# Summing q's shift row by one matmul of a high and a low part instead of a full-precision matmul, in a one-core transformer block

## The chip, the cores and the metric

The kernel is one launch on one core of a Trainium2 chip. The metric is device time in microseconds (us), the median of the runs shown. The core's engines are TensorE (PE in the rows; its weight loads are PEld), VectorE (DVE), ScalarE (ACT), GpSimd (POOL) and SyncE (SP), each with a queue that is worked off in order, and 16 DMA engines that serve transfers issued by SyncE, ScalarE and GpSimd. Instructions of different engines wait for one another through semaphores.

## The reference

A block of two parts on x with 2048 tokens (S) and 448 channels (D), all in float32. A condition vector c gives six rows of length 448 (shift, scale and gate for each part):

```python
mod = (silu(c) @ w_mod).reshape(1, 6, 1, -1)
sa, ca, ga, sb, cb, gb = (mod[:, i] for i in range(6))
h = layernorm(x) * (1 + ca) + sa
x = x + ga * A(h, wqkv, wo)       # linear attention, 16 heads of 28
h = layernorm(x) * (1 + cb) + sb
x = x + gb * B(h, w1, b1, w2, b2) # MLP over the tokens, 1792 wide
```

In A, q, k and v are h @ wqkv, phi(t) = where(t > 0, t + 1, exp(t)) + 1e-6, kv and z sum phi(k) v and phi(k) over the tokens, and the output is phi(q) kv / (phi(q) z), times wo.

## The kernel before

The 2048 tokens are 16 tiles of 128. float32 products are made of float32r matmuls: an operand is split into a high part (ScalarE's copy to float32r) and a low part (VectorE's difference), and three products high*high, high*low and low*high are added in PSUM. A matmul's moving operand has 448 columns.

**Projection with the norm folded in.** k and q are projected from the raw tile x (transposed by the host, `xt`), with weights scaled by 1 + ca (`Whi`, `Wlo`). Mean, and what the shift sa adds, enter by a last small matmul: `close(t, j)` (line 437) multiplies rows of tile t (mean and standard deviation, brought into place by a transpose on TensorE, `a_transpose`, line 401) with `Wrow[j]`, which holds the column sums of the scaled weights and the **shift row** sa @ W of projection j (j = 1 is k, j = 0 is q).

**How `Wrow[0]` is made.** `row_part(0, ch)` (line 275) adds, on VectorE, the four weight chunks times the shift column into `accb[0]`, [128, 448] float32. `row_sum(0)` (line 283) sums the weights' parts over the partitions by seven matmuls with the selector `sel_s`; `row_bias(0)` (line 289) adds the sum of `accb[0]` over its 128 partitions, by one matmul with float32 operands (`sel_b`, all 128 partitions). `row_out(0)` (line 292) copies the result's rows into `Wrow[0]` by ScalarE (high) and VectorE (low). `close(0, 0)`, q of tile 0, is the first that needs it.

**The order** is the program's own (a manual schedule): each engine gets its instructions in the order in which the code issues them. The loop over t from 4 to 15 (line 682) works on several tiles at once. In turn t, TensorE projects k of tile t+1, closes tile t, adds tile t-4 to the kv sums (`a_outer`, eleven matmuls, tiles `cacc`), transposes rows for tiles t+1 and t+2 (odd t) and, from t = 10 on, projects q of tile t-10 (`a_q`). VectorE and ScalarE take statistics of tile t+3, normalise tile t-2 (`a_norm`: tile `xn`; `a_high`, `a_low`: `xh`, `xl`), form phi(k) of tile t (`pk`), and split tile t+3 (`hh`, `hl`). `a_rows(t+2)` (line 393) writes on VectorE what the transpose reads (`rowst`). The third of the six rows, ga, is made beside it: `mod_part(2, k)`, k = 0 to 3, and `mod_add(2)` on VectorE, `mod_high(2)` on ScalarE and VectorE, then `mod_sum2(2)`, a matmul (tile `modp`), in turn 12.

GpSimd issues transfers that add to a tile in SBUF (`nc.gpsimd.dma_start(..., accum_op=ALU.add)`, lines 528 and 541): the low parts of phi(k), and the running sums of phi(k) for odd and even tiles. SyncE issues all loads. Temporaries come from a pool of 74 equal buffers (`slot`): a new tile takes a freed buffer, and its first writer waits for whoever used the buffer last.

After the loop come the attention output, tile by tile, interleaved with the first group of the MLP's first layer (lines 950 to 952), then the rest of that layer, and the second layer as seven products (lines 1183 and 1184).

Of the kernel before, what the change touches and what calls it, by code (L numbers as in the profile page):

```python
# [8 lines left out]
F32 = mybir.dt.float32  # L9
F32R = mybir.dt.float32r  # L10
AF = mybir.ActivationFunctionType
# [3 lines left out]
P = 128  # L15
S, D, F = 2048, 448, 1792
# [15 lines left out]
ROWS = 98  # L32
# [5 lines left out]
CUT2 = {2: 9, 3: 9, 4: 8, 5: 7}  # L38
LAG = 5
MOD_AT = {11: [(4, 0), (4, 1), (4, 2)], 13: [(4, 3), (4, None), (3, 0), (3, 1)]}  # L40
QS = {0: 3}
WARM = 6
POOL_LOW = (0, 1, 2)
# [8 lines left out]
def block_kernel(ctx: ExitStack, tc: tile.TileContext, x, xt, wqkv, wo, w1, b1, w2, c, wmod, wfirst, out):  # L52
    nc = tc.nc
# [5 lines left out]
    cst = ctx.enter_context(tc.tile_pool(name="cst", bufs=1))  # L59
# [16 lines left out]
    def moving(new, name, dt=F32R, parts=P):  # L76
        return new(name, dt=dt, parts=parts, w=512)[:, 16:16 + D]
# [22 lines left out]
        nc.gpsimd.affine_select(out=m3, in_=m3, compare_op=ALU.is_ge, fill=0.0, base=DH - 1,  # L100
                                pattern=[[0, 4], [DH, 4], [0, DH]], channel_multiplier=-1)

    cst.tile([P, 112], F32, name="space")
    mhalf = cst.tile([P, 2], F32, name="mhalf")
    nc.vector.memset(mhalf, -0.5)
    roots = cst.tile([P, 2], F32, name="roots")
# [2 lines left out]
    sel_b = cst.tile([P, ROWS], F32, name="sel_b")  # L109
# [3 lines left out]
    for i in (64, 66, 96):  # L113
        nc.gpsimd.memset(sel_f[:, i:i + 1], -1.0)
        nc.gpsimd.memset(sel_b[:, i + 1:i + 2], 1.0)
    sel_s = cst.tile([P, ROWS], F32R, name="sel_s")
    rowst = []
    for i in range(RING):
        rowst.append(cst.tile([P, P], F32R, name=f"rowst{i}"))
# [107 lines left out]
    def mod_part(j, k):  # L227
        if k == 0:
            macc[j] = (tslot if j == 5 else slot)(f"acc{j}", parts=G)
            nc.vector.tensor_scalar_mul(macc[j], wm[j, 0], sc[:G, 0:1])  # L230
        else:
            nc.vector.scalar_tensor_tensor(macc[j], wm[j, k], sc[:G, k:k + 1], macc[j], op0=ALU.mult, op1=ALU.add)


    def mod_add(j):
        acc = macc[j]
        nc.vector.tensor_add(acc[:G - 64], acc[:G - 64], acc[64:])

    def mod_high(j):
        acc, both = macc[j], moving(slot, f"mh{j}")  # L240
        macc[j] = (both,)
        nc.scalar.activation(both[:64], acc[:64], AF.Copy)
        return lambda: nc.vector.tensor_sub(both[64:], acc[:64], both[:64].bitcast(F32))
# [12 lines left out]
    Whi, Wlo, Wrow, rowb, accb = {}, {}, {}, {}, {}  # L256
# [18 lines left out]
    def row_part(j, ch):  # L275
        if ch == 0:
            accb[j] = slot(f"accb{j}")
            nc.vector.tensor_scalar_mul(accb[j], raw_w[j, 0], col[0][:, 0:1])
        else:
            nc.vector.scalar_tensor_tensor(accb[j], raw_w[j, ch], col[0][:, ch:ch + 1], accb[j],  # L280
                                           op0=ALU.mult, op1=ALU.add)

    def row_sum(j):
        rowb[j] = bank(f"rowb{j}")
        ws = [Whi[j, ch] for ch in range(4)] + [Wlo[j, ch] for ch in range(3)]
        for i, w in enumerate(ws):
            nc.tensor.matmul(rowb[j][:ROWS, :D], sel_s, w, start=(i == 0), stop=False)  # L287

    def row_bias(j):
        nc.tensor.matmul(rowb[j][:ROWS, :D], sel_b, accb.pop(j), start=False, stop=True)  # L290

    def row_out(j):
        ps, w = rowb.pop(j), Wrow[j]
        nc.scalar.activation(w[64:ROWS], ps[64:ROWS, :D], AF.Copy)
        nc.vector.tensor_sub(w[96:ROWS], ps[96:ROWS, :D], w[96:ROWS].bitcast(F32))
# [155 lines left out]
    def a_exp(t, ps):  # L451
        a_exp1(t, ps)
        a_relu(t, ps)
# [31 lines left out]
    def a_phi_q(keep=0):  # L485
        a_exp_q(keep)
        for t in sorted(eqs):
            pq[t] = phi_q(t)
# [191 lines left out]
    wo_sb = []  # L680
    late = [t for t in range(NT) if t not in Q_EARLY.values()]
    for t in range(4, NT):
        if 5 < t < NT - 1:
            project(t + 1, 1, "kp")
        kp = close(t, 1) if t > 4 else kps[4]
        if t == 9:
            row_sum(0)
            row_bias(0)
        if t > 4:
            a_outer(t - KV_LAG)  # L690
        if t % 2 and 4 < t < NT - 2:
            a_transpose(t + 1)
        if t in Q_EARLY:
            a_q(Q_EARLY[t])
        if t == 12:
            mp = mod_sum2(2)
        pair = t % 2 and 7 < t + 3 < NT
        if pair:
            first, second, end = a_stats_dve((t + 3, t + 4))
            first(0)  # L700
        if 5 <= t < 9:
            w_low(0, t - 5)
        if pair:
            second(0)
        if 5 <= t < 9:
            row_part(0, t - 5)
        a_phi_q(t in Q_EARLY)
        if t == 9:
            a_exp(t, kp)
        if t % 2 and 4 < t < NT - 2:  # L710
            a_copy(t + 1)
            a_copy(t + 2)
        if t != 9:
            a_exp(t, kp)
        if 7 < t + 3 < NT:
            a_split_high(t + 3)
        a_pk_parts(t - 1)
        highs = HIGH_AT.get(t, (t - 2,))
        for i in highs[:1]:
            a_norm(i)  # L720
            a_high(i)
        if t % 2 == 0 and 4 < t < NT - 3:
            low = a_rows(t + 2)
        if t == 11:
            low2 = mod_high(2)
        for j, i in MOD_AT.get(t, ()):
            mod_add(j) if i is None else mod_part(j, i)
        if t == 14:
            low4()
        a_pk(t, kp)  # L730
        if t % 2 == 0 and 4 < t < NT - 3:
            low()
        if 7 < t + 3 < NT:
            a_split_low(t + 3)
        for i in highs[1:]:
            a_norm(i)
            a_high(i)
        if pair:
            first(1)
        for i in highs:  # L740
            a_low(i)
        if pair:
            second(1)
            end()
        sum_end()
        if 4 <= t < 8:
            w_high(0, t - 4)
            if t == 7:
                w_row(0)
        if t == 9:  # L750
            row_out(0)
        if t == 12:
            mod_out(2, mp)
            make_mask()
        if t in FETCH:
            load_xt(FETCH[t])
            load_x(FETCH[t])
        if 7 <= t < 11:
            mod_part(2, t - 7)
        if t == 10:  # L760
            mod_add(2)
        if t == 11:
            low2()
        if t == 13:
            low4 = mod_high(4)
        if t in (7, 10):
            load_mod(4 if t == 7 else 3)
        if t == 10:
            load_qkv(2, tslot)
        if t == 8:  # L770
            for g in range(4):
                w = tslot(f"wo{g}", parts=G)
                nc.sync.dma_start(w, wo[g * G:(g + 1) * G, :])
                wo_sb.append(w)
            b12 = cst.tile([P, NF + NT], F32, name="b12")
            nc.sync.dma_start(b12, b1)
            b1c, b2c = b12[:, :NF], b12[:, NF:]
        if t >= 13:
            nc.vector.tensor_mul(wo_sb[t - 13], wo_sb[t - 13], mods[2][:G])
        load_to(PRE_LOAD.get(t, 0))  # L780
# [34 lines left out]
    for ch in range(4):  # L815
        for g in range(4):
            s = slice(g * G, (g + 1) * G)
            nc.tensor.matmul(kvb[:G, s], raw_w[2, ch][:, s], csum[ch][:, s], start=(ch == 0 and g == 0),  # L818
                             stop=(ch == 3), skip_group_check=True)
# [168 lines left out]
    for i in range(NT + LAG):  # L988
# [11 lines left out]
        t = i - LAG  # L1000
# [386 lines left out]
```

## Time and profile before

| what | before |
|---|---|
| median of 3 runs | 433.62 us (433.53 to 434.19) |
| the profiled execution | 434.09 us |
| its span, first to last instruction | 432.4 us |
| TensorE matmul busy | 427.9 us (99%) |
| VectorE busy | 365.1 us (84%) |
| ScalarE busy | 278.9 us (65%) |
| GpSimd busy | 120.1 us (28%) |
| moved by DMA | 66.14 MB, mean 153 GB/s |

The span is 1.69 us shorter than the profiled execution's time; what lies around the span is no instruction of the program. Times inside the profile count from the first instruction. In a row of the timeline stand the start, the duration, the engine, the source line, the operation, the tile written and those read, the shapes, the count, and in brackets how long the engine was idle before it and what ended that. Consecutive matmuls overlap in these rows (their ends are modelled), so their spacing is read from the starts.

### The profile page before, as it was taken

How to read it: one execution, taken by the hardware profiler on the slowest of the kernel's cores; microseconds unless marked ns; L12 is line 12 of the kernel's file. 1: busy time of each engine (PE TensorE's matmuls, PEld its weight loads, DVE VectorE, ACT ScalarE, POOL GpSimd, SP SyncE). 2: the span in 40 equal slices, each digit the busy share in tenths (PEclk: the TensorE clock that was granted, in tenths of full speed). 3: DMA queues.
4: the chain of work that ended last, by engine and by line, in shares of the span. 5: the costliest groups of instructions: out<-in, count | busy, mean ns of one | idle time of the engine just before them, and what ended most of it. 6: DMA issues, size and time to landing. Idle time of an engine off the chain costs nothing.

```text
span 432.4 us, 7216 instructions
## 1 busy us (share of the span) xinstructions
PE 427.9 (99%) x2331; PEld 398.0 (92%) x2331; DVE 365.1 (84%) x814; ACT 278.9 (65%) x595; POOL 120.1 (28%) x199
## 2 busy tenths in 40 slices
PE   8999999999999999999999999999999999999997
PEld 8888899999899999999999999999999999999996
DVE  4899987889899999998579695739799998898894
ACT  5799869658578899996755263537464664655550
POOL 4345444300026577775200000010113131132010
PEclk9999999999999999999999999999999999999999
DMA  8997997565300036354427461577379977986431
GB/s 282 385 337 162 239 264 162 89 206 193 86 1 0 26 74 148 74 125 97 145 85 244 142 212 50 166 203 210 79 193 214 207 159 159 214 170 144 85 46 41
DMA packets 63797, 66.14 MB, mean 153 GB/s; under 512 B 4816, under 2 KB 55312, under 8 KB 63760
## 3 DMA queue, kind: packets, MB, share of 16 engines
q1 hardware_dynamic: 54688, 50.90, 37.8%
q0 software_dynamic: 8784, 14.32, 20.8%
q10 hardware_dynamic: 288, 0.46, 0.4%
q8 instruction: 18, 0.29, 0.3%
q14 instruction: 19, 0.16, 0.1%
HBM read 46.30 MB, written 7.34 MB: 124 GB/s over the span
## 4 chain that ended last, share of the span: by engine, by line
PE 97%; DVE 1%; ACT 1%; issue 0%
PE y L1183 19%; PE up L951 10%; PE up L950 10%; PE up L952 10%; PE y L1184 9%; PE cacc L554 7%; PE qp L432 7%; PE op L893 7%; PE kp L432 6%; PE op L900 1%; PE warm L188 1%; PE tq L863 1%; PE qp L439 1%; PE kvb L818 1%; PE wp L968 1%; PE rowb L287 1%
## 5 line engine op out<-in xcount | busy, mean ns | idle before, releaser
L950 PE MATMUL up<-h2h,ph 128*128 128x448 f32 x224 | 81.2, 362 | 0.0
L951 PE MATMUL up<-h2l,ph 128*128 128x448 f32 x224 | 81.2, 362 | 0.0
L952 PE MATMUL up<-h2h,pl 128*128 128x448 f32 x224 | 80.8, 361 | 0.0
L1138 POOL DMA_DIRECT2D a<-a x16 | 14.2, 964 | 142.6 <-DMA pr<-in_B_w_dram 76.7
L950 PEld LDWEIGHTS up<-h2h,ph 128*128 128x128 f32 x224 | 42.0, 188 | 3.1
L952 PEld LDWEIGHTS up<-h2h,pl 128*128 128x128 f32 x224 | 41.9, 187 | 3.0
L951 PEld LDWEIGHTS up<-h2l,ph 128*128 128x128 f32 x224 | 42.0, 188 | 2.3
L84 DVE TENSOR_TENSOR pl<-pr,ph 128x512 fp32r<-128x512 f32 x46 | 30.7, 688 | 2.6 <-ACT ph L83 1.7
L1189 ACT ACTIVATE cc<-y 128x448 f32<-128x448 f32 x24 | 13.0, 546 | 26.7 <-PE y L1184 26.7
L1102 DVE TENSOR_TENSOR u<-u,mod 128x448 f32<-128x448 f32 x14 | 8.7, 623 | 23.0 <-ACT u L1101 22.8
L83 ACT ACTIVATE ph<-pr 128x512 fp32r<-128x512 f32 x46 | 27.6, 623 | 0.8 <-PE up L952 0.5
L1101 ACT ACTIVATE u<-up,b 128x448 f32<-128x448 f32 x14 | 8.8, 625 | 25.4 <-PE up L952 24.9
L432 PE MATMUL kp<-wh,hh 128*128 128x448 f32 x64 | 23.8, 377 | 0.0
L554 PE MATMUL cacc<-pkh,xh 128*128 128x448 f32 x64 | 23.6, 369 | 0.0
L432 PE MATMUL qp<-wh,hh 128*128 128x448 f32 x64 | 23.5, 368 | 0.0
L1203 POOL DMA_DIRECT2D out_dram<-yt x14 | 12.7, 909 | 37.3 <-DVE yt L1194 27.9
L843 POOL TENSOR_SCALAR den<-den 128x16 f32<-128x16 f32 x16 | 8.8, 548 | 44.2 <-DVE den L840 44.2
L554 PE MATMUL cacc<-pkl,xh 128*128 128x448 f32 x56 | 20.3, 362 | 0.0
L893 PE MATMUL op<-wph,pth 128*128 128x448 f32 x48 | 18.7, 390 | 0.0
L1144 DVE TENSOR_TENSOR a<-a,s 128x512 f32<-128x512 f32 (+1 forms) x32 | 18.5, 622 | 0.0
L83 ACT ACTIVATE s2h<-s 128x512 fp32r<-128x512 f32 (+1 forms) x16 | 8.3, 569 | 15.5 <-DVE s L1144 15.5
L1183 PE MATMUL y<-ub,a11h 128*128 128x448 f32 x56 | 18.2, 375 | 0.0
(235 smaller groups left out, 1383.7 us busy)
## 6 DMA issues: line engine op xcount, KB each, us to landing
pr<-in_B_w_dram SPq DMA_DIRECT2D x56, 256.0 KB, 3.1
a<-in_B_w_dram SPq DMA_DIRECT2D x32, 256.0 KB, 4.8
a<-in_B_w_dram SPq DMA_DIRECT2D x32, 192.0 KB, 4.7
xt<-in_xt_dram SPq DMA_DIRECT2D x16, 256.0 KB, 5.0
x<-in_A_x_dram SPq DMA_DIRECT2D x16, 224.0 KB, 5.0
wm<-in_B_wmod_dram SPq DMA_DIRECT2D x16, 196.0 KB, 5.2
out_dram<-x SPq DMA_DIRECT2D x14, 224.0 KB, 2.3
out_dram<-yt POOLq DMA_DIRECT2D x14, 224.0 KB, 6.1
```

The lines of the kernel that those rows point to most:

```text
L83: nc.scalar.activation(hi, full, AF.Copy)
L84: nc.vector.tensor_sub(lo, full, hi.bitcast(F32))
L432: nc.tensor.matmul(pps[t, j][:, :D], a[:, ch * P:(ch + 1) * P], w, start=first, stop=False)
L554: nc.tensor.matmul(cacc[ch][:, :D], a[:, s], b, start=(t == 0 and i == 0), stop=(t == NT - 1 and i == len(todo) - 1))
L893: nc.tensor.matmul(opb[t][:, :D], a, b, start=(ch == n == 0), stop=False)
L950: nc.tensor.matmul(ps[:, :D], hi[:, sl], mh, start=first, stop=False)
L951: nc.tensor.matmul(ps[:, :D], hi[:, sl], ml, start=False, stop=False)
L952: nc.tensor.matmul(ps[:, :D], lo[:, sl], mh, start=False, stop=last)
L1138: nc.gpsimd.dma_start(w, a, accum_op=ALU.add)
L1144: nc.vector.tensor_tensor(w, raw2[q, a][i], raw2[q, b][i], op=op)
L1183: nc.tensor.matmul(ps[:, :D], h[:, s], w, start=opens and r == 0, stop=False, skip_group_check=True)
L1184: nc.tensor.matmul(ps[:, :HD], l[:, s], wh, start=False, stop=closes and r == PAIRS - 1, skip_group_check=True)
```

## The change

`accb[0]` is no longer summed by the float32 matmul. In turn 8, after the last `row_part(0, 3)`, `row_fold(0)` adds, on VectorE, partitions 64 to 127 of `accb[0]` to its partitions 0 to 63 (64x448). In turn 9 `row_high(0)` copies the 64 partitions' high part by ScalarE into a new tile `rb0` (float32r, rows 0 to 63), copies the selector to float32r (`sel_r`, also ScalarE), and VectorE writes the low part into rows 64 to 127. `row_bias(0)` becomes one float32r matmul of `sel_r` with `rb0`. Its place and that of `row_sum(0)` move from turn 9 (after `close(9, 1)`) to the start of turn 10, ahead of the projection of tile 11; `row_out(0)` moves from the end of turn 9 to turn 10, after `close(10, 1)`. The steps `mod_part(2, 1..3)` and `mod_add(2)` move from turns 8, 9, 10 and 10 to turns 9, 10, 11 and 11. The spacer tile in the constants' pool shrinks by what `sel_r` takes. k's shift row (j = 1) stays as it was.

```diff
+PARTS = (7, 9, 10)
...
-    cst.tile([P, 112], F32, name="space")
+    cst.tile([P, 14], F32, name="space")
...
+    sel_r = cst.tile([P, ROWS], F32R, name="sel_r")
...
     def row_bias(j):
-        nc.tensor.matmul(rowb[j][:ROWS, :D], sel_b, accb.pop(j), start=False, stop=True)
+        nc.tensor.matmul(rowb[j][:ROWS, :D], sel_r if j == 0 else sel_b, accb.pop(j), start=False, stop=True)
+
+    def row_fold(j):
+        acc = accb[j]
+        nc.vector.tensor_add(acc[:64], acc[:64], acc[64:])
+
+    def row_high(j):
+        acc, both = accb[j], moving(slot, f"rb{j}")
+        nc.scalar.activation(both[:64], acc[:64], AF.Copy)
+        nc.scalar.activation(sel_r, sel_b, AF.Copy)
+        accb[j] = both
+        return lambda: nc.vector.tensor_sub(both[64:], acc[:64], both[:64].bitcast(F32))
...
     for t in range(4, NT):
+        if t == 10:
+            row_sum(0)
+            row_bias(0)
         if 5 < t < NT - 1:
             project(t + 1, 1, "kp")
         kp = close(t, 1) if t > 4 else kps[4]
-        if t == 9:
-            row_sum(0)
-            row_bias(0)
+        if t == 10:
+            row_out(0)
...
         if 5 <= t < 9:
             row_part(0, t - 5)
+            if t == 8:
+                row_fold(0)
         a_phi_q(t in Q_EARLY)
         if t == 9:
             a_exp(t, kp)
+            row_high(0)()
...
         if t == 11:
+            mod_part(2, 3)
+            mod_add(2)
             low2 = mod_high(2)
...
-        if t == 9:
-            row_out(0)
...
-        if 7 <= t < 11:
-            mod_part(2, t - 7)
-        if t == 10:
-            mod_add(2)
+        if t in PARTS:
+            mod_part(2, PARTS.index(t))
```

The order of the instructions on three stretches, before and now; numbers behind a name are buffers, and in brackets stand the semaphores that an instruction waits for (DVE is VectorE's own, DMASW are GpSimd's transfers). Line numbers of the changed kernel are 2 to 16 higher.

VectorE in turn 8, before: the last part of the shift row, then `xn` of tile 6, the two writes of `rowst` for tile 10's transpose, `mod_part(2, 1)` (`acc`), and the statistics of tile 12.

```order
L280 SCALAR_TENSOR_TENSOR accb_561<-wr_3_175,col_199,accb_561 128x448
L496 TENSOR_SCALAR xn_770<-x_167,mv_486 128x448
L395 CAST rowst_105<-mv_677 128x4x2 [waits Pool_49]
L458 SCALAR_TENSOR_TENSOR pk_776<-ek_758,rk_759 128x448 [waits Activation_49]
L398 TENSOR_TENSOR rowst_105<-mv_677,rowst_105 128x2x2 [waits DVE_49]
L415 TENSOR_TENSOR hl_763<-xt_536,hh_762 128x512 [waits DMAHW3_49,Activation_49]
L505 TENSOR_TENSOR xh_772<-xn_770,xh_772 128x64 [waits DMASW6_49,DMASW5_49,Activation_49]
L506 TENSOR_TENSOR xl_773<-xn_770,xh_772 128x384
L232 SCALAR_TENSOR_TENSOR acc_723<-wm_1_374,sc,acc_723 112x448 [waits DMAHW6_49]
L380 BN_STATS st_830<-x_597 128x6 [waits DMAHW6_49]
L383 BN_AGGR mv_828<-st_830 128x2 [waits DVE_49]
L496 TENSOR_SCALAR xn_847<-x_179,mv_486 128x448
```

The same stretch now:

```order
L282 SCALAR_TENSOR_TENSOR accb_562<-wr_3_176,col_200,accb_562 128x448
L296 TENSOR_TENSOR accb_562<-accb_562 64x448 [waits DVE_49]
L509 TENSOR_SCALAR xn_772<-x_168,mv_487 128x448 [waits DVE_49]
L408 CAST rowst_106<-mv_678 128x4x2 [waits Pool_49]
L471 SCALAR_TENSOR_TENSOR pk_778<-ek_760,rk_761 128x448 [waits Activation_49]
L411 TENSOR_TENSOR rowst_106<-mv_678,rowst_106 128x2x2 [waits DVE_49]
L428 TENSOR_TENSOR hl_765<-xt_537,hh_764 128x512 [waits DMAHW3_49,Activation_49]
L518 TENSOR_TENSOR xh_774<-xn_772,xh_774 128x64 [waits DMASW6_49,DMASW5_49,Activation_49]
L519 TENSOR_TENSOR xl_775<-xn_772,xh_774 128x384
L393 BN_STATS st_822<-x_598 128x6 [waits DMAHW6_49]
L396 BN_AGGR mv_820<-st_822 128x2 [waits DVE_49]
L303 TENSOR_TENSOR rb_829<-accb_562,rb_829 64x448 [waits Activation_49]
```

The fold (L296) stands ahead of `rowst`, with a wait for VectorE's own last result before and behind it; the low part of `rb0` (L303) stands behind tile 12's first statistics; `mod_part(2, 1)` is gone from here.

TensorE around the row matmuls, before: after tile 9's close, the seven sums, the float32 matmul, and the first kv matmul of tile 5 (ten more follow, and then the transpose `rw` and tile 11's projection).

```order
L287 MATMUL rowb_806<-wh_3_715,sel_s 98x448 [waits DVE_49]
L287 MATMUL rowb_806<-wl_0_558,sel_s 98x448
L287 MATMUL rowb_806<-wl_1_622,sel_s 98x448
L287 MATMUL rowb_806<-wl_2_681,sel_s 98x448
L290 MATMUL rowb_806<-accb_561,sel_b 98x448 [waits DVE_49]
L554 MATMUL cacc_437<-pkh_632,xh_701 128x448
```

Now they stand behind tile 5's kv matmuls and the transpose:

```order
L567 MATMUL cacc_441<-pkl_634,xh_702 128x448
L417 MATMUL rw_818<-ident,rowst_106 98x128 [waits DVE_49]
L289 MATMUL rowb_864<-wh_0_535,sel_s 98x448 [waits Activation_49]
L289 MATMUL rowb_864<-wh_1_594,sel_s 98x448
L289 MATMUL rowb_864<-wh_2_651,sel_s 98x448
L289 MATMUL rowb_864<-wh_3_716,sel_s 98x448
L289 MATMUL rowb_864<-wl_0_559,sel_s 98x448
L289 MATMUL rowb_864<-wl_1_623,sel_s 98x448
L289 MATMUL rowb_864<-wl_2_682,sel_s 98x448
L292 MATMUL rowb_864<-rb_829,sel_r 98x448 [waits DVE_49,Activation_49]
L445 MATMUL kp_873<-wh_0_223,hh_764 128x448
```

Eight matmuls moved back behind eleven others and the transpose, so those twelve come earlier; the transpose waits for `rowst`, the last row matmul for `rb0`.

VectorE in turn 11, before: phi(q) of tile 0, `xn` of tile 9, three parts of the fifth row (`mod_part(4, 0..2)`), phi(k) of tile 11, and the rest of the turn.

```order
L470 SCALAR_TENSOR_TENSOR pq_998<-eq_994,rq_995 128x448 [waits PE_49,Activation_49]
L496 TENSOR_SCALAR xn_1014<-x_370,mv_554 128x448
L230 TENSOR_SCALAR acc_1021<-wm_0_725,sc 112x448 [waits DMAHW1_49,PE_49]
L232 SCALAR_TENSOR_TENSOR acc_1021<-wm_1_727,sc,acc_1021 112x448 [waits DMAHW2_49,DVE_49]
L232 SCALAR_TENSOR_TENSOR acc_1021<-wm_2_729,sc,acc_1021 112x448 [waits DVE_49]
L458 SCALAR_TENSOR_TENSOR pk_1025<-ek_1002,rk_1003 128x448 [waits PE_49,Activation_49]
L415 TENSOR_TENSOR hl_1007<-xt_865,hh_1006 128x512 [waits DMAHW2_49,Activation_49]
L380 BN_STATS st_1028<-x_932 128x6 [waits DMAHW5_49]
L505 TENSOR_TENSOR xh_1016<-xn_1014,xh_1016 128x64 [waits DMASW6_49,DMASW5_49,Activation_49]
```

Now:

```order
L483 SCALAR_TENSOR_TENSOR pq_1002<-eq_998,rq_999 128x448 [waits PE_49,Activation_49]
L509 TENSOR_SCALAR xn_1018<-x_371,mv_555 128x448 [waits DMASW6_49,DMASW5_49]
L234 SCALAR_TENSOR_TENSOR acc_724<-wm_3_379,sc,acc_724 112x448
L239 TENSOR_TENSOR acc_724<-acc_724 48x448 [waits DVE_49]
L232 TENSOR_SCALAR acc_1027<-wm_0_726,sc 112x448 [waits DMASW1_49,DMAHW1_49,DVE_49,PE_49]
L234 SCALAR_TENSOR_TENSOR acc_1027<-wm_1_728,sc,acc_1027 112x448 [waits DMAHW2_49,DVE_49]
L234 SCALAR_TENSOR_TENSOR acc_1027<-wm_2_730,sc,acc_1027 112x448 [waits DVE_49]
L471 SCALAR_TENSOR_TENSOR pk_1031<-ek_1006,rk_1007 128x448 [waits Activation_49]
L428 TENSOR_TENSOR hl_1011<-xt_859,hh_1010 128x512 [waits DMAHW2_49,Activation_49]
```

Two steps of the third row came in ahead of the fifth's. And since the buffers of the pool fall to other tiles, the wait for GpSimd's transfers DMASW6 and DMASW5 (phi(k) of tile 9 added to the odd tiles' sum, and its low part) has gone from `xh` of tile 9, seven places further on, to `xn` of tile 9 itself.

## Prediction

> **What bounds the kernel now.** I read the page's busy times and its chain first: which engine is full, and whose work ended last.
>
> ```profile
> PE 427.9 (99%) x2331; PEld 398.0 (92%) x2331; DVE 365.1 (84%) x814; ACT 278.9 (65%) x595; POOL 120.1 (28%) x199
> ...
> PE 97%; DVE 1%; ACT 1%; issue 0%
> ```
>
> TensorE is busy for 99% of the span and makes up 97% of the chain. Then the waits of TensorE, the whole view:
>
> ```profile
> PE warm L188 <- DVE roots L108: 1.1, 1, 1.1
> PE rw L404 <- ACT rk L449: 0.2, 1, 0.2
> ```
>
> Two waits, 1.3 us in all. So a microsecond that TensorE saves or loses in the middle is saved or lost at the end, unless a wait moves in. Next, TensorE's own rows at the place (starts; a long row merges its count).
>
> ```profile
> 48.90 0.97 PE L287 MATMUL rowb<-wh,sel_s 128*98 128x448 f32 x4
> ...
> 50.32 0.91 PE L290 MATMUL rowb<-accb,sel_b 128*98 128x448 f32 x2
> ...
> 51.27 0.37 PE L554 MATMUL cacc<-pkl,xh 128*128 128x448 f32 x1
> ...
> 53.29 0.27 PE L404 MATMUL rw<-ident,rowst 128*98 128x128 f32 x1
> ...
> 53.60 0.36 PE L432 MATMUL kp<-wl,hh 128*128 128x448 f32 x1
> ```
>
> The seven float32r sums take 50.32 - 48.90 = 1.42 us, 0.20 each. The float32 matmul (two rows) and the first kv matmul end at 51.27, so 0.95 - 0.20 = 0.75 for the float32 one. Ten more kv matmuls bring us from 51.27 to 53.29: eleven are 2.22. Transpose and one matmul are 0.31, the transpose 0.11; the first matmul of tile 11's projection stands at 53.60 - 0.20 = 53.40.
>
> The engine that feeds TensorE here is VectorE; its timeline in turn 8:
>
> ```profile
> 49.01 0.69 DVE L280 SCALAR_TENSOR_TENSOR accb<-wr,col,accb 128x448 f32<-128x448 f32 x1
> 49.61 0.51 DVE L496 TENSOR_SCALAR xn<-x,mv 128x448 f32<-128x448 f32 x1
> ...
> 50.64 0.16 DVE L398 TENSOR_TENSOR rowst<-mv,rowst 128x4 fp32r<-128x4 f32 x1
> ...
> 51.45 0.55 DVE L506 TENSOR_TENSOR xl<-xn,xh 128x384 fp32r<-128x384 f32 x1
> 51.92 0.68 DVE L232 SCALAR_TENSOR_TENSOR acc<-wm,sc,acc 112x448 f32<-112x448 f32 x1
> 52.51 0.62 DVE L380 BATCH_NORM_STATS2 st<-x 128x6 f32<-128x448 f32 x1
> 53.17 0.18 DVE L383 BATCH_NORM_AGGREGATE mv<-st 128x2 f32<-128x6 f32 x1
> ```
>
> No row carries an idle time: VectorE works without a pause here, so whatever is put in delays all that stands behind it. `rowst`, which the transpose reads, is complete at 50.80, and the transpose runs at 53.29: a lead of 2.5 us, most of it because the row matmuls stand in between.
>
> **The change part by part.** *The saved matmul.* One float32r matmul replaces 0.75 by 0.20: TensorE gains 0.55 us. No other TensorE work is added. That alone would put tile 11's first matmul at 53.40 - 0.55 = 52.85.
>
> *The row matmuls go behind the transpose.* Tile 5's kv matmuls start at 48.90 and end their turn at 48.90 + 2.22 = 51.12, where the transpose is due.
>
> *The fold on VectorE.* Two later stretches of VectorE show its price and that of everything behind (turns 10 to 12):
>
> ```profile
> 61.00 0.68 DVE L232 SCALAR_TENSOR_TENSOR acc<-wm,sc,acc 112x448 f32<-112x448 f32 x1
> 61.72 0.62 DVE L237 TENSOR_TENSOR acc<-acc 48x448 f32<-48x448 f32 x1
> ...
> 63.54 0.51 DVE L496 TENSOR_SCALAR xn<-x,mv 128x448 f32<-128x448 f32 x1
> 64.44 0.45 DVE L230 TENSOR_SCALAR acc<-wm,sc 112x448 f32<-112x448 f32 x1 [0.40 <-PE cacc L554]
> 64.93 1.41 DVE L232 SCALAR_TENSOR_TENSOR acc<-wm,sc,acc 112x448 f32<-112x448 f32 x2
> 66.54 0.62 DVE L458 SCALAR_TENSOR_TENSOR pk<-ek,rk 128x448 f32<-128x448 f32 x1 [0.20 <-ACT rk L449]
> 67.08 0.69 DVE L415 TENSOR_TENSOR hl<-xt,hh 128x512 fp32r<-128x512 f32 x1
> 67.69 0.62 DVE L380 BATCH_NORM_STATS2 st<-x 128x6 f32<-128x448 f32 x1
> 69.04 0.23 DVE L505 TENSOR_TENSOR xh<-xn,xh 128x64 fp32r<-128x64 f32 x1 [0.73 <-ACT xh L500]
> ...
> 70.06 0.62 DVE L243 TENSOR_TENSOR mh<-acc,mh 64x448 fp32r<-64x448 f32 x1
> 70.71 0.63 DVE L470 SCALAR_TENSOR_TENSOR pq<-eq,rq 128x448 f32<-128x448 f32 x1
> ```
>
> `mod_add` (L237) is the same kind of fold: 0.62 us, started 0.04 after the end of what it reads. `row_fold` then runs from 49.01 + 0.69 + 0.04 = 49.74 to 50.36, and `xn`, which now waits for it, starts at 50.40 instead of 49.61: 0.79 later, and so does all behind it. The moved `mod_part(2, 1)` gives nothing back here, as it stood behind `rowst`. So `rowst` is complete at 50.80 + 0.79 = 51.59, after 51.12.
>
> What a late operand costs TensorE shows in turn 1 of the kv sums: the chain, then TensorE's rows.
>
> ```profile
> 30.19 0.48 DVE xl L506
> 30.67 0.04 issue
> ```
>
> ```profile
> 30.71 0.47 PE L554 MATMUL cacc<-pkh,xl 128*128 128x448 f32 x1
> 31.02 0.37 PE L554 MATMUL cacc<-pkh,xh 128*128 128x448 f32 x1
> ```
>
> The matmul starts 0.04 after VectorE's result, and the next follows after 0.31 instead of 0.20: I count 0.05 and then 0.10. The transpose starts at 51.64 and has lost 51.64 + 0.10 - 51.12 = 0.62 us. With 0.11 for itself and 1.42 for the sums, the last row matmul is due at 53.27.
>
> *The low part of `rb0`.* Its form is L243's (64x448, written to the upper partitions): 0.62, starting 0.03 after its forerunner. `xl` of tile 6 starts at 51.45 + 0.79 = 52.24; the statistics follow after 0.47 (their place, 51.92, is free of `mod_part`) at 52.71; the aggregate after 0.66 at 53.37, to 53.55; the low part runs from 53.58 to 54.20. ScalarE must have written the high part by then. Its rows:
>
> ```profile
> 50.17 0.56 ACT L500 ACTIVATE xh<-xn 128x448 fp32r<-128x448 f32 x1
> 50.63 0.62 ACT L446 ACTIVATE ek<-kp,mv 128x448 f32<-128x448 f32 x1
> 51.15 0.63 ACT L449 ACTIVATE rk<-kp,mv 128x448 f32<-128x448 f32 x1
> ```
>
> `xh` waits for the later `xn` (50.91) and starts at 50.94; two steps on, 52.44, the high part starts and takes L242's 0.56 (below): 53.00, in time. The selector's copy (98 columns, under those 0.56) ends before 53.6 and is hidden too. So the last row matmul starts at 54.25 instead of 53.27: 0.98, and 0.10, lost. Tile 11's first matmul is at 54.25 + 0.10 + 0.20 = 54.55 against 53.40. **Up to here the change loses 1.15 us**: 0.62 + 1.08 - 0.55.
>
> The Trainium skill, page "TensorE: Matmul & The Clock Gate", section "Step-by-step: what each phase is for", says that TensorE can load the next weights ahead of matmuls still in flight. For the last row matmul and `modp` the late operand is the moving one, so the 0.10 would vanish there; the two rows above had late weights, and no run here shows the other case. By it the whole forecast sum below would be 0.2 lower.
>
> *What moves in turns 10 to 12.* `row_out` moves, but q of tile 0 closes only after the projections of tile 11, tile 6's kv matmuls and its own projection: over thirty matmuls of 0.20, about 6 us after the sums. `mod_part(2, 3)` and `mod_add(2)` come into turn 11, and `xn` of tile 9 now waits for the transfer that adds phi(k) of tile 9 to a running sum. When that lands is seen where ScalarE waited for it, with GpSimd's issue:
>
> ```profile
> 68.43 0.58 ACT L500 ACTIVATE xh<-xn 128x448 fp32r<-128x448 f32 x1 [0.32 <-DMA pk<-pk]
> 68.91 0.56 ACT L242 ACTIVATE mh<-acc 64x448 fp32r<-64x448 f32 x1
> ```
>
> ```profile
> 61.01 0.86 POOL L541 DMA_DIRECT2D pk<-pk  x1
> ```
>
> Issued at 61.01, landed by 68.43. Before, `xn` of tile 9 ran at 63.54 and only `xh`, late in the turn, had to wait. Now VectorE stands still until the landing, and queued behind are both third-row steps, the fifth row's three, `pk`, `hl`, statistics and, last, the low part `mh` of the third row, for which TensorE waits in turn 12. From the start of `xn` to the end of `mh`, by the spacings above: 0.42 + 0.72 + 0.65 + 0.49 + 1.33 + 1.15 + 0.54 + 1.02 + 0.62 = 6.94 us (`xn`; part; fold; the fifth row's first; its other two; `pk` and `hl`; statistics; `xh` to `mh`; `mh`). At a landing of 68.43 `mh` ends at 75.37. TensorE's row:
>
> ```profile
> 73.43 0.36 PE L253 MATMUL modp<-mh,ones_r 128*128 128x448 f32 x1
> ```
>
> It is due at 73.43 + 1.15 = 74.58, and would start at 75.42 and lose another 0.94. If the transfer lands by 67.5, nothing is lost. GpSimd issues it at the same time as before, since ScalarE's `pkl` of tile 9 comes no later; but SyncE's loads of these microseconds, which share the DMA engines, are held up behind the later VectorE, so it may land somewhat sooner. Between the ends 0 and 0.94 I take half, 0.47. **Sum: 1.15 + 0.47 = 1.6 us lost.**
>
> After that nothing is late:
>
> ```profile
> 75.00:432.00 357.00, 354.34 (x1978) 332.02 (x1977) 301.97 (x647) 219.66 (x474) 86.96 (x144) 1.00 0.52 130
> ```
>
> From 75 us on VectorE (third, 301.97 of 357) has 15% to catch up in, and TensorE is nearly full. The clock (1.00) stays.
>
> On the profiled execution's 434.09 (span 432.4, 1.69 around it) the sum gives 435.7; on the median of the runs, 433.62, which is the scale of the forecast, 435.2.
>
> **The rivals.** *Two waits only.* The sum transfer lands by 67.5, and the third wait never comes: +1.15, 434.8. For it: loads start later. Against: the row itself, 7.4 us from issue to landing. The Trainium skill, page "DMA: Bandwidth & Descriptors", section "Anatomy of one DMA — SWDGE (gpsimd) path", prices such a transfer at 2.0 us plus its bytes at 436 GB/s; for 229 KB that is an estimate of 2.5 us, which would land at 63.5 and give this rival's time. The row speaks against that price.
>
> *Not slower: VectorE is ahead.* If in the timed runs `rowst` is there by 51.07 and the low part of `rb0` by 52.60 (due at 51.12 + 0.11 + 1.42 = 52.65), no wait comes and the 0.55 stays: 433.1. It decides at 1.6 us: VectorE would need that much lead over what I worked out. Against: no idle row between 49.01 and 53.17 to draw it from.
>
> *A draw.* VectorE is about 1.2 us ahead of my count, or the waits swallow just the gain: 433.6. For: the profiled execution itself is 0.47 longer than the median, and may stretch VectorE.
>
> *Worse.* The transfer lands after 68.43, or the late VectorE makes TensorE wait once more after turn 12: 436.0 and up.
>
> That the new matmul isn't cheaper can be left out: both operands are float32r as in the seven sums, with 0.20 each in the rows.
>
> **How the numbers follow.** Three waits (434.9 to 435.9): 0.52. Two waits: 0.20. Ahead: 0.10. Draw: 0.09. Worse: 0.09. The forecast is 435.2. The range leaves out "ahead" and "worse": 433.4 to 436.0. 0.2%, about what can be told from no change, is 0.87 us: slower begins at 434.49. Slower: 0.52 + 0.12 of "two waits" + 0.09 = 0.73. Within: 0.08 of "two waits" + 0.09 + 0.07 of "ahead" = 0.24. Faster: 0.03.
>
> **What would show it.** In the changed kernel's waits TensorE should wait for VectorE's `rowst` (0.4 to 0.6 us), then for `rb` (about 1), and at `modp` for `mh` (0 to 0.9); VectorE should be idle before `xn` of tile 9 until a transfer has landed at about 68; the last row matmul should be one row, with 0.20 to the next. The prediction is wrong if TensorE's waits stay empty, or if VectorE's `rowst` is complete before 51.1.

## The result and the profile after

| | median of runs, us | ratio to before, 95% interval |
|---|---|---|
| before | 433.62 (433.31 to 434.19, 5 runs) | |
| changed | 437.79 (437.57 to 438.33, 5 runs) | 1.0093 [1.0079, 1.0107] |

The change costs 4.2 us, where 1.6 were forecast and the range ended at 436.0. TensorE's first matmuls run at a slow pace for longer in some executions than in others (last section), which moves a time by up to about 1 us, so kernels are compared below by their traces as well: from the first matmul of tile 10's projection (46.70 us in the trace of before) to the end of TensorE's last one (429.34). That distance is 382.64 us before and 386.92 after.

The page of the changed kernel, busy times and chain:

```profile
PE 430.0 (99%) x2330; PEld 395.5 (91%) x2330; DVE 366.2 (84%) x816; ACT 280.0 (64%) x597; POOL 120.2 (28%) x199
...
PE 83%; DVE 7%; DMA 6%; ACT 2%; issue 1%; POOL 0%; DVEq 0%; ACTq 0%
```

TensorE is as full as before (99%), but its busy time has risen by 2.1 us with one matmul row fewer: something there takes longer. The waits of TensorE:

```profile
PE warm L190 <- DVE roots L109: 1.1, 1, 1.1
PE rowb L292 <- DVE rb L303: 0.9, 1, 0.9
PE modp L255 <- DVE mh L245: 0.5, 1, 0.5
PE rw L417 <- DVE rowst L411: 0.2, 1, 0.2
```

Beside the wait at the warm-up, which before has too, these are the three waits that were forecast, and no others. TensorE's rows at the place, in the timeline of the changed kernel:

```profile
46.15 0.37 PE L445 MATMUL kp<-wh,hh 128*128 128x448 f32 x1
...
50.40 0.37 PE L567 MATMUL cacc<-pkl,xh 128*128 128x448 f32 x1
50.99 0.32 PE L417 MATMUL rw<-ident,rowst 128*98 128x128 f32 x1 [0.21 <-DVE rowst L411]
51.06 1.07 PE L289 MATMUL rowb<-wh,sel_s 128*98 128x448 f32 x4
51.97 0.77 PE L289 MATMUL rowb<-wl,sel_s 128*98 128x448 f32 x3
53.69 0.42 PE L292 MATMUL rowb<-rb,sel_r 128*98 128x448 f32 x1 [0.95 <-DVE rb L303]
53.94 0.37 PE L445 MATMUL kp<-wh,hh 128*128 128x448 f32 x1
...
74.04 0.37 PE L452 MATMUL qp<-wrow,hl 98*128 98x448 f32 x1
74.91 0.44 PE L255 MATMUL modp<-mh,ones_r 128*128 128x448 f32 x1 [0.50 <-DVE mh L245]
75.19 0.37 PE L445 MATMUL kp<-wh,hh 128*128 128x448 f32 x1
```

The transpose was due at 50.40 + 0.20 = 50.60 and starts 0.39 late; the last row matmul was due at 51.97 + 0.60 = 52.57 and starts 1.12 late; `modp` was due at 74.24 and starts 0.67 late. (The waits view and the brackets count from the modelled end of the matmul before, so each shows about 0.17 less.) VectorE's rows behind them:

```profile
49.08 0.62 DVE L296 TENSOR_TENSOR accb<-accb 64x448 f32<-64x448 f32 x1
49.74 0.51 DVE L509 TENSOR_SCALAR xn<-x,mv 128x448 f32<-128x448 f32 x1
...
50.77 0.16 DVE L411 TENSOR_TENSOR rowst<-mv,rowst 128x4 fp32r<-128x4 f32 x1
...
52.92 0.62 DVE L303 TENSOR_TENSOR rb<-accb,rb 64x448 fp32r<-64x448 f32 x1
...
67.80 0.51 DVE L509 TENSOR_SCALAR xn<-x,mv 128x448 f32<-128x448 f32 x1 [2.67 <-DMA pk<-pk]
...
74.14 0.62 DVE L245 TENSOR_TENSOR mh<-acc,mh 64x448 fp32r<-64x448 f32 x1
```

The fold takes its 0.62 ahead of `xn`; `rowst` is complete at 50.93 and the low part of `rb0` at 53.54, 0.06 and 0.15 ahead of the matmul that waited; `xn` of tile 9 stands still for 2.67 us until the transfer has landed at 67.8, and `mh` ends at 74.76.

What the waits don't hold is in the windows view. From turn 13, behind the third wait, to the last 0.4 us the changed kernel has this row (length; TensorE's busy time and count come first):

```profile
76.50:435.70 359.20, 356.57 (x1979) 332.21 (x1977) 303.36 (x653) 220.89 (x477) 88.29 (x146) 1.00 0.53 130
```

Before, the same stretch (75.00 to 432.00, shown above) took 357.00 with 1978 rows of TensorE. At the same granted clock, without a wait, the same work takes 2.2 us more. The starts show where. Tile 12's projection and the kv sums behind it in the changed kernel:

```profile
60.67 0.37 PE L445 MATMUL kp<-wh,hh 128*128 128x448 f32 x1
...
62.93 0.37 PE L567 MATMUL cacc<-pkh,xh 128*128 128x448 f32 x1
...
65.14 0.27 PE L417 MATMUL rw<-ident,rowst 128*98 128x128 f32 x1
```

The same in the kernel before:

```profile
60.03 0.36 PE L432 MATMUL kp<-wh,hh 128*128 128x448 f32 x1
...
62.24 0.36 PE L554 MATMUL cacc<-pkh,xh 128*128 128x448 f32 x1
...
64.45 0.27 PE L404 MATMUL rw<-ident,rowst 128*98 128x128 f32 x1
```

In the changed kernel the eleven matmuls of the first stretch (ten of the projection, and tile 11's close) take 2.26, 0.2055 each, and the eleven of the kv sums 2.21, 0.2009 each; before it is 2.21 and 2.21. The same holds for all matmuls with these weights (0.2053 against 0.2007 in the q projections, the mean of 168 and 169 pairs of starts). The first MLP layer's keep 0.2000 in both, save 36 of its 672 (last section).

The projections read resident weights, `Whi` and `Wlo`, as their moving operand. Nothing in the diff touches them, but they have moved: the constants' tiles are laid out in steps of 32 bytes, so the spacer shrinks from 448 bytes to 64 (14 columns are 56), by 384, and `sel_r` (98 columns, 392 bytes) takes 416. Everything behind, the resident weights too, starts 32 bytes further on. The first weight lies at byte 168576 of its partitions before, 168608 after.

### The profile page after: what moved, and what is told of

Read it like the earlier page. It is cut to its first block, busy times and chain, and to the rows that moved or that the text cites. A ratio compares the mean times of both kernels' runs of the same rounds, so it can differ in the third digit from the quotient of the medians.

```text
span 436.1 us, 7220 instructions
## 1 busy us (share of the span) xinstructions
PE 430.0 (99%) x2330; PEld 395.5 (91%) x2330; DVE 366.2 (84%) x816; ACT 280.0 (64%) x597; POOL 120.2 (28%) x199
## 4 chain that ended last, share of the span: by engine, by line
PE 83%; DVE 7%; DMA 6%; ACT 2%; issue 1%; POOL 0%; DVEq 0%; ACTq 0%
PE y L1199 19%; PE up L966 10%; PE up L968 10%; PE up L967 10%; PE y L1200 9%; PE op L909 7%; PE qp L445 6%; PE cacc L567 4%; DMA xt<-in_xt_dram 2%; DMA wr<-in_qkv_dram 2%; DMA pk<-pk 2%; PE op L916 2%; PE kp L445 1%; PE tq L879 1%; DVE hl L428 1%
```

## The experiments

To the end means from tile 10's projection to TensorE's end; to tile 14, from there to the first matmul of tile 14's projection, at 73.63 in the trace of before, just behind `modp` (the three waits lie in it). The expectations below call that projection tile 13's; by the code turn 12 projects tile 13, at 66.78, and the one behind `modp` is tile 14's.

| run | median, us | ratio [95%] | to tile 14 | to the end |
|---|---|---|---|---|
| before | 433.5 to 433.9 | | 26.93 | 382.64 |
| changed | 437.79 | 1.0093 [1.0079, 1.0107] | 29.04 | 386.92 |
| changed, old addresses | 436.14 | 1.0046 [1.0032, 1.0060] | 28.86 | 384.55 |
| before + 32 bytes | 435.90 | 1.0056 [1.0043, 1.0069] | 27.26 | 385.14 |
| before + 64 | 435.19 | 1.0041 [1.0027, 1.0055] | 27.14 | 384.39 |
| before, pool + 32 | 435.82 | 1.0044 [1.0031, 1.0056] | 27.19 | 384.29 |
| before, both + 32 | 433.99 | 1.0006 [0.9997, 1.0014] | 26.95 | 382.67 |
| fold late | 435.97 | 1.0054 [1.0042, 1.0066] | 29.10 | 384.79 |
| parts early | 435.06 | 1.0035 [1.0023, 1.0048] | 30.96 | 386.66 |
| parts early, again | 435.17 | 1.0035 [1.0025, 1.0044] | 28.01 | 383.72 |
| rows mid | 433.60 | 1.0005 [0.9996, 1.0014] | 27.02 | 382.71 |
| rows mid, fold late | 433.55 | 1.0001 [0.9992, 1.0010] | 27.09 | 382.79 |
| before + 128 | 434.61 | 1.0020 [1.0010, 1.0030] | 27.10 | 383.57 |
| before, moving at 80 | 437.33 | 1.0089 [1.0073, 1.0104] | 27.27 | 386.52 |
| split | 433.26 | 0.9992 [0.9983, 1.0000] | 26.45 | 382.15 |
| before + 256 | 433.41 | 0.9994 [0.9985, 1.0002] | 26.94 | 382.63 |

**The changed kernel at the old addresses.**

```diff
-    cst.tile([P, 14], F32, name="space")
+    cst.tile([P, 6], F32, name="space")
```

> The changed kernel with a spacer of 6 columns in place of 14, which puts every tile behind the selectors back to the address that it had before the change (they stood 32 bytes further on). Theory (address): in the changed kernel the k projections of tiles 11 to 15 are spaced 0.205 us instead of 0.201, while the kv sums keep 0.200; the matmuls that read a resident weight as moving operand are slower because that weight starts 32 bytes past a multiple of 64. 530 such matmuls in the program by 0.0045 are 2.4 us, the second layer's about 0.4 more: 437.8 - 2.8 = 435.0, with TensorE's three waits (rowst, rb, mh) as they are. Rival (other buffers, or what the waits set off later): the address changes nothing, 437.8, spacing 0.205.

The spacing of the projections is back at 0.2006 (168 pairs), and to the end it is 2.37 us shorter than the changed kernel. Its waits near the change:

```profile
PE rowb L292 <- DVE rb L303: 1.0, 1, 1.0
PE modp L255 <- DVE mh L245: 0.6, 1, 0.6
PE rw L417 <- DVE rowst L411: 0.3, 1, 0.3
```

The three waits are there as in the changed kernel, and alone, with the saved matmul set against them, they cost 384.55 - 382.64 = 1.91 us. The median, 436.14, is above the 435.0 expected; its five runs lie at 434.92 to 435.26 (two) and 436.14 to 436.28 (three), as the two starts would part them; its profiled execution had the long one.

**The kernel before, moved by 32 and by 64 bytes.**

```diff
-    cst.tile([P, 112], F32, name="space")
+    cst.tile([P, 120], F32, name="space")
```

> The kernel before with a spacer of 120 columns in place of 112: all tiles behind it 32 bytes further on, nothing else. Theory (address): 433.6 + 2.8 = 436.4, spacing of the k projections 0.205, no new wait of TensorE. Rival (other buffers or the waits): 433.6, spacing 0.201.

Tile 12's projection and the kv sums behind it in this run:

```profile
59.46 0.37 PE L432 MATMUL kp<-wh,hh 128*128 128x448 f32 x1
...
61.72 0.37 PE L554 MATMUL cacc<-pkh,xh 128*128 128x448 f32 x1
...
63.94 0.27 PE L404 MATMUL rw<-ident,rowst 128*98 128x128 f32 x1
```

They take 2.26 and 2.22, as in the changed kernel. No wait came, the spacing in the q projections is 0.2054, and to the end it is 2.50 us more: the address alone. With the 1.91 of the waits that makes 4.41, against the 4.28 that the change costs. With 128 columns in the spacer:

```diff
-    cst.tile([P, 112], F32, name="space")
+    cst.tile([P, 128], F32, name="space")
```

> The kernel before with a spacer of 128 columns in place of 112: all tiles behind it 64 bytes further on. Theory (start within 64 bytes): 433.6, spacing 0.201, no difference. Rival (any move of these tiles, or their place within a longer stretch than 64 bytes, costs): 436.4 as with 32 bytes.

Both theories fell: 0.2040, between the two, and 1.75 us more to the end.

**The kernel before, its pool of buffers moved and the weights not.**

```diff
+    pad = ctx.enter_context(tc.tile_pool(name="pad", bufs=1))
+    pad.tile([P, 8], F32, name="pad")
     slots = ctx.enter_context(tc.tile_pool(name="slots", bufs=NSLOT))
...
-    cst.tile([P, 112], F32, name="space")
+    cst.tile([P, 104], F32, name="space")
```

> The kernel before with the pool of 74 buffers and the first constants 32 bytes further on and the resident weights where they were (a tile of 8 columns ahead of the pool, 8 columns less in the spacer). Theory (only the moving operand's start counts): the kv sums (176) and the first MLP layer (672), whose moving operands lie in the pool, are slower by 0.0045 each, 3.8 us, the second layer's matmuls with moving operands in the pool by some 0.3: 437.7; the projections, whose stationary operands lie in the pool, keep 0.201. Rival one (the stationary operand's start counts as well): another 2.4 us for the projections and the attention output, 440.1. Rival two (only the resident weights' tiles have this): 433.6.

All three theories fell. The kv sums and nearly all of the MLP layer, with both operands in the pool, keep 0.2003 and 0.2000; the projections, whose weights stand where they stood and whose stationary operands have moved, go to 0.2057. So it looked as if neither operand's own place counts, but the distance between the two; the next run tests that.

**Both moved.**

```diff
+    pad = ctx.enter_context(tc.tile_pool(name="pad", bufs=1))
+    pad.tile([P, 8], F32, name="pad")
```

> The kernel before with everything (pool, constants, resident weights) 32 bytes further on, by a tile of 8 columns ahead of the pool. In the runs so far the spacing of matmuls went by the distance between the start of the moving operand and that of the stationary one, modulo 128: 0.200 us at 64 (all of before), 0.205 at 32 or 96, 0.204 at 0. Theory (distance): all distances are 64 again, so the projections, the kv sums and the MLP keep 0.200, and the time is that of before, 433.6 (from the first matmul of tile 10's projection to the end 382.6). Rival (the place of each operand by itself): all are 32 past a multiple of 64, at least the 2.3 of the run with the weights moved, 435.9.

Tile 12's projection and the kv sums behind it in this run:

```profile
59.13 0.36 PE L434 MATMUL kp<-wh,hh 128*128 128x448 f32 x1
...
61.34 0.36 PE L556 MATMUL cacc<-pkh,xh 128*128 128x448 f32 x1
...
63.55 0.27 PE L406 MATMUL rw<-ident,rowst 128*98 128x128 f32 x1
```

2.21 and 2.21 as before, 382.67 to the end. Every operand has another address and nothing has changed: the distance rule holds, and each operand's own place is out.

**How far the rule reaches.** Spacers of 144 and of 176 columns, and, in a third run, moving operands that start 20 columns into their buffers:

```diff
-    cst.tile([P, 112], F32, name="space")
+    cst.tile([P, 144], F32, name="space")
```

```diff
-    cst.tile([P, 112], F32, name="space")
+    cst.tile([P, 176], F32, name="space")
```

```diff
-        return new(name, dt=dt, parts=parts, w=512)[:, 16:16 + D]
+        return new(name, dt=dt, parts=parts, w=512)[:, 20:20 + D]
```

> The kernel before with a spacer of 144 columns in place of 112: everything behind it 128 bytes further on, distances of 192. Theory (distance modulo 128): spacing 0.2005 in the projections as before, 433.5, from tile 10's projection to the end 382.6. Rival (the distance counts over a longer stretch, 256 or 512): another spacing, 0.203 to 0.206 and 385.

> The kernel before with a spacer of 176 columns: everything behind it 256 bytes further on, distances of 320. If the spacing depends on the distance modulo 256 (0.2005 at 64, 0.2025 at 192, 0.204 at 0 and 128, 0.2055 at 32 and 96): 0.2005, 433.6, to the end 382.6. If over a longer stretch: 0.2025 or more, 434.6 or more.

> The kernel before with the moving operands 20 columns into their buffers in place of 16: distances of 80 wherever they were 64, in the projections, the kv sums and the first MLP layer alike. If the price rises evenly from 64 to 96, the spacing is 0.2025 everywhere and the time 433.5 + 1382 x 0.0025 = 437; if it is one of steps of 32, 0.2005 as before and 433.5, or 0.205 and 440.

A distance of 192 gave 0.2027 and 0.9 us more to the end, so 128 isn't the period; 320 gave 0.2005 and 382.63, so 256 fits. At 80 it is 0.2033 to 0.2041 for the projections, the kv sums and the MLP layer alike, more than an even rise from 64 to 96 would give and less than a full step.

**The fold behind `rowst`** (from here on at the old addresses).

```diff
-            if t == 8:
-                row_fold(0)
...
             low()
+        if t == 8:
+            row_fold(0)
```

> The changed kernel at the old addresses, with the fold behind the second write of rowst instead of ahead of xn. Theory (waits in series): the transpose no longer waits, but the low part of rb ends when it did, so the last row matmul waits longer by what the transpose waited less: from tile 10's projection to tile 13's 28.9 us as without the edit (28.86; before 26.93). Rival (each wait costs for itself): 28.4. The third wait (mh) should stay, 0.6.

TensorE's waits:

```profile
PE rowb L292 <- DVE rb L303: 1.6, 1, 1.6
...
PE modp L255 <- DVE mh L245: 0.8, 1, 0.8
```

The wait for `rowst` is gone and the one for `rb` is 0.6 longer; the sum is no smaller (29.10 against 28.86). The waits stand in series on one VectorE that is late.

**The third row's last steps in turn 10.**

```diff
         if t == 11:
-            mod_part(2, 3)
-            mod_add(2)
             low2 = mod_high(2)
...
+        if t == 10:
+            mod_part(2, 3)
+            mod_add(2)
```

> The changed kernel at the old addresses, with the third row's last part and fold at the end of turn 10, where VectorE stands idle for 2.7 us, instead of in turn 11. The buffers fall so that xn of tile 9 doesn't wait for GpSimd's transfer. Theory: mh is written over 1.3 us earlier and the third wait goes, from tile 11's projection to tile 13's 20.3 instead of 21.0; the waits for rowst and rb stay; 0.7 less than the run at the old addresses, 434.4 to 435.5. Rival (the third wait comes from the later VectorE as a whole): 21.0 stays.

Inconclusive as a trace: in the execution profiled a transfer landed late, and ScalarE's row and TensorE's behind it were these:

```profile
66.48 0.64 ACT L478 ACTIVATE eq<-qp,mv 128x448 f32<-128x448 f32 x1 [5.89 <-DMA pk<-pk]
```

```profile
67.69 0.47 PE L445 MATMUL qp<-wh,hh 128*128 128x448 f32 x1 [2.62 <-ACT rq L479]
```

That execution took 437.3; the other nine lie between 434.25 and 435.41. So once more:

> The run with the third row's last steps in turn 10 once more, as its profiled execution was 2.2 us above its own median and held a wait of 2.6 us that the median can't hold. Theory: in an ordinary execution the waits for rowst and rb are there, none at modp, and tile 11's to tile 13's projection takes 20.3 (21.0 with the third wait). Rival (the third wait is there in ordinary executions): 21.0.

```profile
PE rowb L292 <- DVE rb L303: 1.0, 1, 1.0
PE rw L417 <- DVE rowst L411: 0.3, 1, 0.3
```

No wait at `modp`, and from tile 11's projection to tile 14's 20.17 instead of 21.01. But the edit takes two things away at once: the two steps have left turn 11, and with other buffers `xn` of tile 9 no longer waits for the transfer and starts at 64.73. The next run tells them apart.

**The row matmuls behind tile 11's projection.**

```diff
-        if t == 10:
-            row_sum(0)
-            row_bias(0)
         if 5 < t < NT - 1:
             project(t + 1, 1, "kp")
+        if t == 10:
+            row_sum(0)
+            row_bias(0)
```

> The changed kernel at the old addresses, with the eight row matmuls behind tile 11's projection (ahead of tile 10's close) instead of ahead of it, 2.05 us more for rb. The buffers fall so that xn of tile 9 doesn't wait for the transfer, but mh itself does. Theory: the wait for rb goes (1.05), that for mh too, since xn starts 2.6 us earlier, and rowst's 0.3 to 0.4 stays: from tile 10's projection to tile 13's 28.86 - 1.05 - 0.7 = 27.1; 433.8 in the median. Rival (waits in series: mh stays late against a TensorE that is now earlier): 28.2 or more, 434.9.

27.02, and no wait for `rb` or `mh`; the one for `rowst` stays. By the starts in the trace the transpose is 0.50 late, the matmul behind it 0.05 more, and `hl` of tile 11 (see the next run) costs 0.15: more than the 0.55 gained. The two steps of the third row stand in turn 11 here, as in the changed kernel, and only `xn` of tile 9 is free of the transfer (it starts at 64.34); `mh` is done at 71.31, 1.6 us before `modp`. So the third wait needs the transfer. That it needs the two steps as well is only worked out: they take 1.43 of VectorE's time in the changed kernel (68.23 to 69.66), for a wait of 0.67. With this edit and that of the fold behind `rowst` together:

> The changed kernel at the old addresses, row matmuls behind tile 11's projection and the fold behind rowst. Theory: none of the three waits is left, so what remains is the cheaper matmul, -0.55, and nothing against it: from tile 10's projection to tile 13's 26.93 - 0.55 = 26.4, the median 433.5 - 0.55 = 432.95. Rival (the fold and the low part on VectorE make something else late): 26.9 or more, 433.5.

The rival was right: 27.09. TensorE's rows show what came in:

```profile
50.71 0.37 PE L445 MATMUL kp<-wl,hh 128*128 128x448 f32 x1
51.53 0.47 PE L445 MATMUL kp<-wh,hl 128*128 128x448 f32 x1 [0.45 <-DVE hl L428]
51.84 0.36 PE L445 MATMUL kp<-wh,hh 128*128 128x448 f32 x1
```

The fold now delays `hl` of tile 11, due at 50.91: 0.62 and 0.11 lost, more than the 0.55 gained. The eight row matmuls had been VectorE's lead.

**The sums where they were, only the one matmul moved.**

```diff
         if 5 < t < NT - 1:
             project(t + 1, 1, "kp")
+        if t == 10:
+            row_bias(0)
         kp = close(t, 1) if t > 4 else kps[4]
+        if t == 9:
+            row_sum(0)
```

> The changed kernel at the old addresses, with the seven sums of the weights back at their old place in turn 9 and only the one matmul of rb moved, behind tile 11's projection; the fold stays where the change put it. Theory: the seven sums stand again ahead of the transpose and give VectorE 1.42 us, so rowst (due 52.5 on the clock of the profile before, complete 51.6), hl of tile 11 (due 53.0, complete 52.2) and rb (due 54.7, complete 53.6) are all in time, and mh too: from tile 10's projection to tile 13's 26.93 - 0.55 = 26.4, to the end 382.1, the median 433.6 - 0.55 = 433.05. Rival (VectorE's work or the new matmul cost TensorE something that isn't seen as a wait): 26.9 and 433.6.

The whole view of TensorE's waits:

```profile
PE warm L190 <- DVE roots L109: 1.1, 1, 1.1
PE kp L445 <- DVE wl L274: 0.2, 1, 0.2
PE rw L417 <- ACT rk L462: 0.2, 1, 0.2
```

No wait is left near the change; 26.45 to tile 14, as expected (26.4), and 0.49 less than before to the end. The ratio, 0.9992 [0.9983, 1.0000], lies at the edge of what runs can tell.

## Why the prediction was wrong

**The saved matmul: right.** 0.55 was forecast; 0.49 came where nothing was late (the split run).

**The wait for `rowst`: right, its size a little over.** Forecast 0.62; the transpose was 0.39 late and 0.07 followed (0.98 us from the transpose to the fifth sum, and 0.91 in the run with the fold late, where the transpose didn't wait). `rowst` was complete at 50.93, which is less than the 51.1 named as a sign of being wrong, but TensorE too is 0.55 earlier in this trace (46.15 against 46.70 for tile 10's projection): on the clock of before it is 51.48.

**The wait for `rb`: right, its size a little under.** Forecast 1.08; 1.12 and 0.05 (53.69 to 53.94). With the gain the forecast was 1.15 lost by tile 11's projection; from tile 10's to tile 11's it is 7.79 against 6.61, 1.18 more, of which the address takes 0.07 (6.68 in the run moved by 32 bytes).

**The third wait: right, its size under.** The 6.94 us from `xn` to the end of `mh` gave 74.74 from a landing at 67.80; the row has 74.76. Forecast 0.47, half of the bound; measured 0.67 (20.58 to 21.25 from tile 11's projection to tile 14's, the moved run against the changed one). The half stood for a transfer that might land sooner, and it didn't: on the clock of before 67.80 is 68.35, against 68.43.

**The step that failed** is "No other TensorE work is added", and with it the end of the sum, "After that nothing is late". It took instructions that the diff doesn't touch at their old duration, and it read the spacer as giving back just what `sel_r` takes. By 32 bytes it doesn't, and 2.50 of the 4.28 us to the end are that: 0.0047 us for each matmul that reads a resident weight, 0.5 in the second MLP layer. Nothing was late; the matmuls themselves were longer. The forecast's own sum, 1.6, stands against 1.91 at the old addresses; that it comes so near is in part luck, as one size was over and two were under.

**The rivals.** "Two waits only" fell: the transfer landed at 67.8, after the 67.5 that it named, and on the clock of before at 68.35. The price that the Trainium skill gives for such a transfer (page "DMA: Bandwidth & Descriptors", section "Anatomy of one DMA — SWDGE (gpsimd) path"), by which it would have landed at 63.5, doesn't hold in this stretch: here it took 7.6 us (issued at 60.17). "Worse" was the right side, but for neither of its reasons. From the Trainium skill's page "TensorE: Matmul & The Clock Gate", section "Step-by-step: what each phase is for", which says that the next weights can be loaded ahead, the prediction worked out 0.2 less, because nothing would follow behind a late moving operand. The rows don't bear that out: 0.05 and 0.08 followed (53.94 and 75.19), and the late matmul itself started 0.15 after VectorE's result (53.54 to 53.69, 74.76 to 74.91) where late weights let it start after 0.06 (50.93 to 50.99). A late moving operand cost 0.20 and 0.23 in all, more than the 0.15 that was counted, so the sum would not have been lower.

## What to carry to other kernels

A spacer tile in a pool is a statement about addresses: when a tile is added, compare the addresses of what lies behind it in the built program, in bytes as they are laid out, and not the columns. When a result is off and the waits are as forecast, compare the spacing of like instructions, kind by kind, from their starts. And a lead that one engine has over another may be made of just the work that a change moves: ask, for each step moved ahead, which later operands lived from its place.

## What the runs showed of the hardware

**TensorE's pace depends on the distance between its operands in SBUF.** Mean spacing of float32r matmuls of 448 columns by the start of the moving operand less that of the stationary one, modulo 256 bytes:

| distance | spacing, us | seen in |
|---|---|---|
| 64 | 0.2000 to 0.2007 | before, but for the row sums; at 320 too |
| 192 | 0.2021 to 0.2027 | before + 128 |
| 80 | 0.2033 to 0.2041 | moving at 80 |
| 0, 128 | 0.2039, 0.2040 | before + 64 |
| 32, 96 | 0.2061, 0.2054 | before + 32 |
| 32, 96 | 0.2057, 0.2051 | before, pool + 32 |

The distances come from the addresses in the built programs. In the runs with the weights moved, the values at 32 and at 0, and in the run with the pool moved the one at 96, are those of 36 matmuls of the first MLP layer whose stationary operands lay among the resident tiles: in one and the same run they were slow while the rest of that layer kept 0.2000. Why is open: that the two reads meet in the memory is only argued. Whether it is the matmul's own weights or those loaded for the next one is nearly untested, as both mostly had the same distance. Five pairs of starts in each run differ, where a matmul at 32 or 96 is followed by weights at 64 from its moving operand: they take 0.2022 and 0.2020 on the mean (before + 32, pool + 32), against 0.2016 for the same five in before. That leans to the next one's weights, on ten pairs. In the second layer, whose matmuls alternate 448 and 224 columns, 32 bytes cost 0.50 of 123.65 us, and in the run with the pool moved it was 0.29 faster; which distances do that wasn't tried.

**The start.** The second group of warm-up matmuls in before, and the first projection:

```profile
6.16 3.36 PE L188 MATMUL warm<-ones 128*128 128x128 f32 x14
9.17 0.72 PE L432 MATMUL kp<-wh,hh 128*128 128x448 f32 x1
```

In the changed kernel:

```profile
6.06 1.83 PE L190 MATMUL warm<-ones 128*128 128x128 f32 x14
7.64 0.45 PE L445 MATMUL kp<-wh,hh 128*128 128x448 f32 x1
```

The same 14 rows (two for each of seven float32 matmuls) take 0.24 us each in the one and 0.13 in the other, at a granted clock of 1.00 in both. Of sixteen profiled executions four had the long form: before, before + 128, the changed kernel at the old addresses, and the fold late. Before moved by 32, 64 and 256 bytes had the short one, and nothing but addresses differs there, which speaks for the execution and not the kernel; that one kernel shows both wasn't seen in traces. The changed kernel's lead of 1.5 us shrinks to 0.55 by tile 10. The Trainium skill, page "TensorE: Matmul & The Clock Gate", section "Part 1: The HAM clock gate (the "warmup" mystery)", says that the clock is raised by a window that runs on by itself and so at a point that differs from run to run. The rows agree that the point differs; the gate itself they don't show, as the granted clock reads 1.00 throughout.
